# Fixed halves for the products, channel tiles added ahead of the logits, and a new order of the pieces

## The chip, the core and the metric

The kernel runs on one core of one Trainium2 chip. The core has a matmul engine (TensorE, PE in the profile; its weight loads are listed as PEld), three engines for elementwise work (VectorE or DVE, ScalarE or ACT, GpSimd or POOL), a sequencer that only issues DMAs (SyncE or SP), and 16 DMA engines. Data is worked on in SBUF, 128 partitions wide; matmuls write to PSUM, eight banks of 512 float32 values per partition. The metric is the device time of one execution in microseconds (us), median of the runs.

## The reference

The input x has 2048 rows of 640 channels. It is normalised, and two branches of it are added to x:

```
xn  = layernorm(x)                                   # per row, eps 1e-5, no scale or shift
A   = attention(xn): q, k, v = xn @ wqkv; 32 heads of 20 channels
      row i looks at rows i, i-2, i-4, ... i-14 (8 window positions, dilation 2)
      logits * 20^-0.5, positions before row 0 masked, softmax over the 8, weighted sum of v, @ wo
B   = gelu(xn @ w1 + b1) @ w2 + b2                   # 640 -> 1536 -> 640, tanh form of gelu
out = x + A + B
```

All inputs and the output are bfloat16.

## The kernel before

**Chunks.** The 2048 rows are worked on as four chunks n = 0 to 3 of 512 rows, each of four blocks of 128 rows. The 640 channels are five tiles of 128, permuted so that the four partitions of a group of 128/32 belong to one head in each of the five tiles; a head's 20 channels are 4 partitions in 5 tiles.

**The pieces of a chunk**, by the names that the order list uses (n is the chunk, further digits count parts):
- `st` (VectorE, L409/L411): mean and variance of one block of x rows, two half rows and one aggregation; `rs` (ScalarE, L430) the square root, `rc` (VectorE, L434/L436) its reciprocal. Block 1 of chunk 0 gets its sum and its sum of squares on ScalarE instead (`sm`, `nm`, `sq`).
- `xn` the normalised rows (VectorE in chunk 0, ScalarE L446 later) and `tc` their transposition into xnT: through TensorE in chunk 0 (`tp`, `tc`), by a transposing DMA on SP later (L477).
- `pj`/`pc`: a projection tile of q, k or v (second digit 0, 1, 2) on TensorE, five matmuls of 512 columns (L509), and its copy out of PSUM on ScalarE (L568). Chunk 0 does this in smaller pieces (`ga` to `ge`, `hj`, with copies `gc`, `hc`). `pad` carries the last 14 columns of k or v into the next chunk.
- `qk` (VectorE, L583): the product of q with k shifted by one window position, all five channel tiles, 2560 elements per partition. Two window positions share one of four rotating buffers `prod`. `lg` (TensorE, L608): sums the products over a head's 20 channels with the 0/1 matrix head_of, into the logits L. For every pair of window positions it runs over 5 channel tiles and 4 blocks, 256 columns each, the four blocks into four 32-partition groups of L: 80 matmuls a chunk.
- the softmax: `mk` mask (chunk 0), `m` maximum, `mx` subtraction, `ss` sums, `ri` reciprocal, `at` weights on VectorE; `ex` exp on ScalarE.
- `xd`, `xs`: DMAs (SP and ScalarE queue) that spread the weights of 32 heads over 128 partitions, into the one buffer ax.
- `av` (VectorE, L681): v times weight, per window position, into the same rotating buffers; `ad` (L690) three additions of 5120 elements and `ot` (L696) one of 2560 give oT.
- `f1`/`ge`: a tile of the hidden layer, five matmuls (L703) and the gelu on ScalarE (L714) into one of 18 buffers hT.
- `o`/`oc`/`od`: an output block of 128 rows, five pieces on TensorE (four of three hidden tiles, the last of the five tiles of oT; L734 for 512 columns, `lo`, L736 for 128, `hi`), the copy to SBUF on ScalarE (L741/L742) and an accumulating DMA on GpSimd (L747) into out. `xp` puts x into out ahead of that and `xb` adds b2. The very last block adds x on VectorE and is stored plainly (`oclo`, `ohi`, `ochi`).

**What sets the order.** Every engine runs its instructions in the order in which they were emitted. The kernel emits the pieces in the order of the list `ORDER`, for PE, DVE, ACT and SP; GpSimd's order is left to the framework. The framework puts in the waits: a piece waits for what it reads, and for the last reader of a buffer that it overwrites. PSUM has four `acc` buffers for projections and hidden tiles, two banks for L and two for lo/hi. The class Plan only names the pieces, their times and needs; the list itself is fixed.

**Loads.** SP issues, in this order, x block 0, wq, wk, x blocks 2 and 3, wv, x blocks 4 to 7, x blocks 8 to 15, w1 in two halves; `ld` later brings w2, wo and b2. Ten matmuls on constants keep TensorE busy until the first data is there.

Of the kernel before, what the change touches and what calls it, by code (L numbers as in the profile page):

```python
# [10 lines left out]
ACT = mybir.ActivationFunctionType  # L11
# [4 lines left out]
PE, VE, SE, DQ, GQ = "pe", "ve", "se", "dq", "gq"  # L16


class Plan:

    TABLE = 1.3
    LAG = {PE: 0.22, VE: 0.08, SE: 0.1, DQ: 0.0, GQ: 0.0}

    def __init__(self, offsets):  # L30
        self.offsets = offsets
        self.tasks, self.by, self.bufs, self.pools = [], {}, {}, {}

    def offset(self, name):
        kind = name[: 4 if name[:2] in ("pj", "pc", "ad") else 3]
        return self.offsets.get(kind, 0.0) + (self.offsets.get(name, 0.0) if name != kind else 0.0)

    def pool(self, name, n):
        self.pools[name] = n

    def add(self, name, engine, us, rank, needs, fn, bufs=(), after=0.0, table=None, slack=0.0, hold=0.0):
        t = {
            "name": name,
            "eng": engine,
            "us": us,
            "rank": rank + self.offset(name),
            "needs": list(needs),
            "fn": fn,
            "bufs": list(bufs),
            "after": after,  # L50
            "table": table,
            "slack": slack,
            "hold": hold,
            "i": len(self.tasks),
        }
        self.tasks.append(t)
        self.by[name] = t
        for b in bufs:
            self.bufs.setdefault(b, set()).add(name)
        return name  # L60

# [12 lines left out]
RD = float(D) ** -0.5  # L74
# [4 lines left out]

COLS = ((0, 2), (2, 4), (4, 5))  # L80
PERIOD = 52.0


ORDER = """
pad01 pad02 st00a st00 sm rs00 me nm rc00 sq xn00a xn00b tp00a tp00b tc00a rs01 tb ga tc00b rc01 xn01 gb2 b1 tp01
gb3 tc01a tc01b gb4 gd gc0 ge st03a hj101 gc4 st03 st02a rs03 hj102 st02 hc101 hj100 rs02 hc102 rc02 rc03 gc1 hj200
xn03 xn02 hc100 st11a tp03 tp02 st13a tc03 hj201 st11 tc02 st10a hj202 hc200 st12a hj012 st10 hj010 st13 hc012 hc202
st12 hj111 hc010 hc201 hj011 rs1 hc111 rc1 st21a hj110 hc011 st22a st22 hj112 hc110 st20a hj212 st33a hc112 f102
xn10 qk031 hc212 f100 xn13 tc10 qk001 ge02 f109 qk020 hj210 pad11 tc13 ge09 hj211 qk010 xn11 f108 hc211 qk000 ge00
f101 tc11 qk011 f105 ge01 ge08 qk021 f104 xn12 f1011 tc12 ge04 qk030 f1010 ge011 st23a st21 lg00 ge010 st20 ld lg01  # L90
ge05 st23 lg02 lg03 st31a rs2 pj114 mk m0 pj102 pc114 st32a st30a pj110 pc102 mx0 hc210 pj111 pc110 st32 ex0 pj101
rc2 st31 st30 pj100 st33 pj112 ss0 pc100 pc101 pj104 xn21 ri0 pj103 tc21 pc104 at0 pc111 pj113 pc103 pc112 pj123
pc113 xn23 qk120 f113 pc123 tc23 xn22 f103 qk111 pj121 ge03 qk121 f118 xd0 qk130 ge13 f107 ge18 f112 qk100 ge07
pad21 f106 ge12 qk110 xs0 f115 ge06 qk131 xw0 f110 rs3 qk101 o020 tc22 xn20 o021 ge15 lg10 lg11 av011 lg12 pc121
tc20 lg13 ge10 rc3 pj120 av000 o022 pc120 av031 xn32 o023 pj122 tc32 av021 f111 pc122 m1 xn30 pj124 ge11 av030 tc30
pad12 pj214 av020 pj204 pc214 pj203 pc204 av001 pj211 pc203 av010 pc124 pj202 xn33 mx1 pc211 pj210 tc33 xn31 ad01
pj221 pc210 pc202 pj223 tc31 pj201 ad00 pj220 pc201 pc223 pj213 xp0 pj200 pc213 ad02 pc221 pj212 pc220 pc200 pj224
pc212 ex1 xb0 ot0 pj310 f1110 qk231 pc310 o024 qk220 pj300 oc02 ss1 pad31 od02 o000 o001 qk200 o002 o003 ri1 o004
at1 pj313 qk201 xd1 oc00 o010 pc313 qk211 pc300 pj301 xs1 qk210 o011 o012 qk221 o013 xw1 pj303 qk230 o014 xp1 xb1
lg20 oc01 lg21 av130 pc303 lg22 pc224 lg23 av100 o030 f138 av110 o031 od00 ge38 av111 pj312 o032 pc301 m2 ge110 f117  # L100
pc312 av131 f116 av120 pj304 pj302 mx2 o033 pc302 av121 ge16 f121 ge17 ad11 f1111 xp2 f1210 ge21 xb2 ge111 o034
ge210 av101 pad22 pc304 f119 ad10 pj311 pj222 pc311 xb3 oc03 pj314 ad12 ge19 od01 f114 od03 f125 ge14 pc222 ot1
pj324 pad32 pc314 ex2 o100 qk331 pj322 qk321 o101 ge25 o102 ss2 o103 pj323 ri2 o104 qk330 pc323 pc322 pj320 at2 oc10
pj321 pc320 qk311 xd2 xs2 o110 pc324 qk301 o111 pc321 o112 qk310 f120 qk300 f126 xw2 f130 ge26 qk320 f127 xl lg30
ge27 lg31 av201 lg32 lg33 o113 m3 o114 av211 f1311 oc11 av200 od11 o120 o121 od10 av221 o122 av230 o123 o124 av220
f1211 oc12 mx3 od12 o130 av210 o131 ge20 ge30 f124 ex3 ad20 f123 o132 ge311 o133 av231 o134 ge24 ss3 f128 ge211 oc13
f129 ad21 ge23 f122 ge29 ge28 f131 ge22 ri3 o210 at3 f135 ad22 o211 xd3 f134 f1310 ot2 o212 ge310 ge31 o213 xs3 o214
xw3 f137 oc21 ge34 od21 o220 av311 o221 o222 av300 o223 av310 o224 f136 av321 oc22 od22 o230 av301 o231 od13 o232
av320 o233 av331 o234 av330 f132 oc23 od23 o200 ad31 o201 ge32 ge36 o202 ge37 f139 ad30 f133 ge39 ge35 o203 ge33
o204 ad32 o310 oc20 o311 o300 ot3 o301 o302 o303 o304 o312 oc30 o313 od30 o320 od20 o321 o322 o323 o314 o324 oc31  # L110
od31 o330 oc32 o331 od32 o332 o333 o334 ohi oclo ochi
""".split()


def make_plan(fns, offsets={}):

    pl = Plan(offsets)
    for name, n in (
        ("acc", 4), ("L", 1), ("O", 1), ("xnT", 3), ("q", 2), ("k", 2), ("v", 2), ("prod", 4),
        ("e", 1), ("attn", 1), ("ax", 1), ("oT", 1), ("hT", 18), ("osb", 2), ("xn", 2), ("m", 1), ("rs", 1), ("ss", 1), ("stats", 4), ("bw", 2),  # L120
    ):
        pl.pool(name, n)

    def f(kind, *a):
        return lambda: fns[kind](*a)

    def turned(n, pair=None):
        if n:
            return [f"tc{n}{bl}" for bl in range(BPC)]
        every = ["tc00a", "tc00b", "tc01a", "tc01b", "tc02", "tc03"]  # L130
        return every if pair is None else every[4 * pair : 4 + 4 * pair]

    def done(n, which):
        if n:
            return [f"pc{n}{which}{to}" for to in range(KT)]
        return (["gc0", "gc1", "gc4"] if which == 0 else [f"hc{which}0{g}" for g in range(len(COLS))]) + [
            f"hc{which}1{g}" for g in range(len(COLS))
        ]

    pl.add("tb", PE, 0.1, -99, ["tp00b"], f("tb"))  # L140
    pl.add("b1", VE, 0.1, -90, ["tb"], f("b1"))
    for n in range(NCH):
        base = n * PERIOD
        prev = base - PERIOD
        early = base + (-37.0 if n == 1 else -85.0)
        xnT, q, k, v, oT = (("xnT", n), ("q", n), ("k", n), ("v", n), ("oT", n))
        hTs = [("hT", n, ft) for ft in range(FT)]

        for bl in range(BPC):
            land = (3.2, 3.65, 9.3, 9.3)[bl] if n == 0 else (0.0, 13.3, 17.6, 17.6)[n]  # L150
            r = -40 if n else -90
            if n == 0 and bl == 1:
                pl.add("sm", SE, 0.84, -99, [], f("sum1"), after=land)
                pl.add("nm", SE, 0.22, -99, ["sm"], f("neg1"))
                pl.add("me", VE, 0.12, -98, ["sm"], f("mean1"))
                pl.add("sq", SE, 0.93, -99, ["nm"], f("sq1"))
                pl.add("rs01", SE, 0.3, -99, ["sq"], f("sqrt", 0, 1, 2), table="sqrt")
                pl.add("rc01", VE, 0.16, -99, ["rs01", "me"], f("rstd", 0, 1, 2))
                continue
            pl.add(f"st{n}{bl}a", VE, 0.42, r, [], f("st", n, bl, 0), [("stats", n, bl)], land)  # L160
            pl.add(f"st{n}{bl}", VE, 0.65, r, [f"st{n}{bl}a"], f("st", n, bl, 1), [("stats", n, bl)], 7.9 if n == 0 and bl == 2 else 0.0)
            if n == 0:
                pl.add(f"rs{n}{bl}", SE, 0.3, -100, [f"st{n}{bl}"], f("sqrt", n, bl, bl + 1), table="sqrt")
                pl.add(f"rc{n}{bl}", VE, 0.16, -99, [f"rs{n}{bl}"], f("rstd", n, bl, bl + 1))
        if n > 0:
            pl.add(f"rs{n}", SE, 0.3, -98, [f"st{n}{bl}" for bl in range(BPC)], f("sqrt", n, 0, BPC), table="sqrt")
            pl.add(f"rc{n}", VE, 0.25, early + -4.0, [f"rs{n}"], f("rstd", n, 0, BPC))
# [18 lines left out]
        if n == 1:  # L186
            pl.add("ld", DQ, 9.2, -1000, turned(1), f("ld"))
# [623 lines left out]
```

## Time and profile before

| | us |
|---|---|
| median of 3 runs | 213.07 (212.35, 213.07, 219.66) |
| span of the profiled execution, first to last instruction | 210.6 |
| its own time | not listed; the lowest run is 1.7 above the span |
| PE busy | 205.5 |
| DVE busy | 173.4 |
| ACT busy | 111.7 |
| POOL busy | 19.8 |
| last matmul ends | 207.9 |

The page gives busy time per engine, then the span cut into 40 slices with the busy share in tenths. The chain that ended last is followed back from the last instruction, at each step to what released it. A group's row reads: line, engine, operation, output from inputs, shapes, count, then busy time and mean nanoseconds of one, then the idle time of the engine ahead of it and what ended most of it. A row of the timeline reads: start, duration, engine, line, operation, output from inputs, count, and in brackets the idle time before. The granted TensorE clock was 1.00 over the whole span. PEld's busy time overlaps PE's.

### The profile page before, as it was taken

Reading aid. Unit: us, or ns where it says so; the run is one execution under the profiler, and the core shown is the slowest. Engines: PE = TensorE matmul, PEld = TensorE weight load, DVE = VectorE, ACT = ScalarE, POOL = GpSimd, SP = SyncE. Lnnn points to the kernel's source line nnn. Section 1 sums busy time; section 2 is a strip of 40 time slices with the busy share of each in tenths; the row PEclk is TensorE's granted clock in tenths of the full one; section 3 lists DMA queues with packets and bytes.
Section 4 is the critical chain, followed back from the end, with each engine's and each line's share of the span. In section 5 each row is a group of like instructions: output and inputs, shape, how many; then the busy total and the mean of one; then the engine's idle time right before and its main releaser. Section 6 shows DMA issues by size and latency. Waiting matters only on the chain.

```text
span 210.6 us, 3645 instructions
## 1 busy us (share of the span) xinstructions
PE 205.5 (98%) x1511; PEld 118.5 (56%) x1535; DVE 173.4 (82%) x178; ACT 111.7 (53%) x193; POOL 19.8 (9%) x37
## 2 busy tenths in 40 slices
PE   8999999999999999999999999999999999999994
PEld 2999656554465555555654555565554455555552
DVE  3587998969979999997899999989999829997001
ACT  5576977889786748330727487321396221441120
POOL 2000000000000002110400600101101011101130
PEclk9999999999999999999999999999999999999999
DMA  6999416924932173569296690621122571212224
GB/s 221 364 363 372 90 33 188 382 56 82 142 72 42 20 187 34 93 94 224 79 150 218 93 156 3 139 93 13 24 29 34 100 127 21 24 27 31 31 21 75
DMA packets 24072, 23.93 MB, mean 114 GB/s; under 512 B 9080, under 2 KB 21880, under 8 KB 24056
## 3 DMA queue, kind: packets, MB, share of 16 engines
q1 hardware_dynamic: 17008, 14.68, 25.1%
q0 software_dynamic: 4144, 4.92, 17.5%
q10 hardware_dynamic: 2904, 4.10, 7.0%
q8 instruction: 12, 0.20, 0.4%
q14 instruction: 4, 0.03, 0.1%
HBM read 10.00 MB, written 7.54 MB: 83 GB/s over the span
## 4 chain that ended last, share of the span: by engine, by line
PE 87%; DMA 7%; SPq 4%; issue 1%; DVE 0%
PE lo L734 27%; PE hps L703 24%; PE pps L509 23%; PE hi L736 8%; DMA w_sb<-in_B_w_dram 7%; PE L L608 4%; SPq L342 2%; SPq L359 2%; PE gps L553 1%; SPq L345 1%; DVE osb L764 0%
## 5 line engine op out<-in xcount | busy, mean ns | idle before, releaser
L703 PE MATMUL hps<-xnT,w_sb 128*128 128x512 bf16 x235 | 55.3, 379 | 0.3
L681 DVE TENSOR_TENSOR pv<-vT,ax 128x2560 bf16<-128x2560 bf16 x32 | 45.8, 1483 | 9.1 <-DMA ax<-attn 4.6
L734 PE MATMUL lo<-w_sb,hT 128*128 128x512 bf16 x184 | 52.9, 379 | 0.1
L583 DVE TENSOR_TENSOR prod<-qT,kT 128x2560 bf16<-128x2560 bf16 x32 | 45.5, 1483 | 1.9 <-ACT kT L568 1.5
L714 ACT ACTIVATE hT<-hps,b1T 128x512 bf16<-128x512 f32 x48 | 31.6, 689 | 18.4 <-PE hps L703 16.9
L736 PE MATMUL hi<-w_sb,hT 128*128 128x128 bf16 x192 | 40.3, 219 | 0.5 <-issue 0.2
L703 PEld LDWEIGHTS <-w_sb 128*128 128x128 bf16 x240 | 22.8, 98 | 26.3 <-DMA w_sb<-in_B_w_dram 0.6
L690 DVE TENSOR_TENSOR pv<-pv 128x5120 bf16<-128x5120 bf16 x12 | 33.7, 2821 | 0.2
L741 ACT CAST osb<-lo 128x512 bf16<-128x512 f32 x15 | 8.8, 587 | 44.7 <-issue 26.7
L734 PEld LDWEIGHTS <-hT 128*128 128x128 bf16 x192 | 18.7, 98 | 22.5 <-issue 0.4
L734 PE MATMUL lo<-wo,oT 128*128 128x512 bf16 x74 | 21.9, 379 | 0.0
L747 POOL DMA_DIRECT2D out_dram<-osb x15 | 13.6, 904 | 86.2 <-ACT osb L742 80.1
L736 PEld LDWEIGHTS <-hT 128*128 128x128 bf16 x192 | 18.4, 98 | 2.7
L509 PE MATMUL pps<-xnT,wk_sb 128*128 128x512 bf16 x73 | 18.2, 379 | 0.1
L509 PE MATMUL pps<-xnT,wv_sb 128*128 128x512 bf16 x72 | 18.0, 379 | 0.1
L509 PE MATMUL pps<-xnT,wq_sb 128*128 128x512 bf16 x75 | 18.0, 379 | 0.1
L736 PE MATMUL hi<-wo,oT 128*128 128x128 bf16 x80 | 16.9, 219 | 0.3
L409 DVE BATCH_NORM_STATS2 stats<-x_sb 128x6 f32<-128x320 bf16 x30 | 13.0, 467 | 4.2 <-DMA x_sb<-in_A_x_dram 4.2
L490 POOL DMA_DIRECT2D out_dram<-b2bc x4 | 5.3, 1465 | 98.6 <-DMA out_dram<-x_sb 98.6
L568 ACT CAST qT<-pps 128x512 bf16<-128x512 f32 x15 | 8.7, 590 | 8.8 <-PE pps L509 8.8
L734 PEld LDWEIGHTS <-oT 128*128 128x128 bf16 x80 | 7.8, 98 | 9.4
L509 PEld LDWEIGHTS <-wk_sb 128*128 128x128 bf16 x75 | 8.6, 118 | 7.3 <-issue 0.2
(75 smaller groups left out, 198.7 us busy)
## 6 DMA issues: line engine op xcount, KB each, us to landing
w_sb<-in_B_w_dram SPq DMA_DIRECT2D x4, 960.0 KB, 11.4
out_dram<-osb POOLq DMA_DIRECT2D x15, 160.0 KB, 3.4
ax<-attn SPq DMA_DIRECT2D x8, 256.0 KB, 4.7
ax<-attn ACTq DMA_DIRECT2D x8, 256.0 KB, 4.3
out_dram<-b2bc POOLq DMA_DIRECT2D x3, 640.0 KB, 6.6
x_sb<-in_A_x_dram SPq DMA_DIRECT2D x1, 1280.0 KB, 14.0
out_dram<-x_sb ACTq DMA_DIRECT2D x1, 1120.0 KB, 4.6
wq_sb<-in_A_wqkv_dram SPq DMA_DIRECT2D x1, 800.0 KB, 4.8
```

The costliest lines, as they stand in the source:

```text
L409: nc.vector.bn_stats(stats[:, i, :], x_sb[:, b, i * (D // 2) : (i + 1) * (D // 2)])
L509: nc.tensor.matmul(ps[:], lhsT=wqkv_p[which][:, ti, to, :], rhs=xnT[:, ti, :], start=(ti == 0), stop=(ti == KT - 1),)
L568: nc.scalar.copy(dest[:, to, off : off + CH], tiles["pps", n, which, to][:])
L583: nc.vector.tensor_tensor(out=prod[:, i, :, :], in0=qkv_tile(n, 0)[:], in1=qkv_tile(n, 1)[:, :, off : off + CH], op=ALU.mult,)
L681: nc.vector.tensor_tensor(out=pv[:, i, :, :].rearrange("p t (j c) -> p t j c", j=BPC), in0=qkv_tile(n, 2)[:, :, off : off + CH].rearrange( ...
L690: nc.vector.tensor_tensor(out=ta[:], in0=ta[:], in1=tb[:], op=ALU.add)
L703: nc.tensor.matmul(ps[:], lhsT=w1_sb[:, ti, ft * P : (ft + 1) * P], rhs=tiles["xnT", n][:, ti, :], start=(ti == 0), stop=(ti == KT - 1),)
L714: nc.scalar.activation(hT[:], tiles["hps", n, ft][:], ACT.Gelu_apprx_tanh, bias=b1T[:, ft : ft + 1], scale=1.0)
L734: nc.tensor.matmul(lo[:], lhsT=lhs, rhs=rhs[:, 0:CH], start=first, stop=last)
L736: nc.tensor.matmul(hi[:, 0 : D - CH], lhsT=lhs, rhs=rhs[:, CH:D], start=first, stop=last)
L741: nc.scalar.copy(osb[:, 0:CH], tiles["lo", n, bl][:])
L747: nc.gpsimd.dma_start(rows, tiles["osb", n, bl][:], accum_op=ALU.add)
```

## The change

Line numbers from here on that name the new kernel say so.

- **Products in fixed halves.** Two fixed buffers `half`, of four window positions each, take the place of the four rotating ones. A product (`qk`, `av`) now covers one block of 128 rows and four window positions: 4 x 5 x 128 = 2560 elements as before. The shifted operand is read through `window`, an access pattern with a step of -2 per window position; the other operand is broadcast.
- **Channel tiles added ahead of the logits.** In chunks 0, 2 and 3, four new VectorE additions `pa` of 2048 elements add channel tiles 1 to 0 and 3 to 2 in the halves; `lg` then runs over tiles 0, 2 and 4 only. A logits matmul has 512 columns (four window positions): 24 in these chunks, 40 in chunk 1. `lg` is one piece that needs all products.
- **Statistics.** For chunks 2 and 3, sum (`su`), negative mean (`ng`) and sum of squares (`sq`) come from ScalarE instead of VectorE. For all rows, the square root and reciprocal are replaced by a tiny VectorE operation (`rc`: variance plus eps) and a power of -0.5 on GpSimd (`rp`, and a product for the bias from chunk 1 on). ScalarE starts with the gelu table loaded.
- **Reuse.** Chunk 3's hidden tiles are written over wq and wk, whose last use is past. In chunks 1 and 3 the spread weights go to the SBUF rows of x blocks 0 to 6, after these were copied to out.
- **Loads.** x blocks 8 to 15 move from ahead of w1 to a piece `ldx` behind chunk 1's transposes, next to w2 (`ld2`); wo and b2 follow in `ldo`.
- **New order.** `ORDER` is another list.

```diff
+    half = [prodp.tile([P, W // 2, KT, CH], BF16, name=f"half{i}") for i in range(2)]
+    def window(src, h, cs):
+        first = PAD - DIL * (W // 2 * h) + cs.start
+        row = src[:, :, first : first + cs.stop - cs.start]
+        (part, n_part), (tile_step, n_tile), (_, n_col) = row.ap
+        return bass.AP(tensor=row.tensor, offset=row.offset,
+            ap=[[part, n_part], [-DIL, W // 2], [tile_step, n_tile], [1, n_col]])
...
+    def do_qk(n, j, h):
+        cs = slice(j * P, (j + 1) * P)
         nc.vector.tensor_tensor(
-            out=prod[:, i, :, :],
-            in0=qkv_tile(n, 0)[:],
-            in1=qkv_tile(n, 1)[:, :, off : off + CH],
+            out=half[h][:, :, :, cs],
+            in0=qkv_tile(n, 0)[:, :, cs].unsqueeze(1).to_broadcast([P, W // 2, KT, P]),
+            in1=window(qkv_tile(n, 1), h, cs),
             op=ALU.mult,
...
+    def do_pa(n, h, c):
+        cs = slice(c * 2 * P, (c + 1) * 2 * P)
+        even, odd = (half[h][:, :, i : KT - 1 : 2, cs] for i in range(2))
+        nc.vector.tensor_tensor(out=even, in0=even, in1=odd, op=ALU.add)
+    def do_lg(n):
+        ts = range(0, KT, 2 if n in PAIRED else 1)      # PAIRED = (0, 2, 3)
+        for t in ts:
+            for h in range(2):
+                for j in range(BPC):
+                    nc.tensor.matmul(
+                        L[j * H : (j + 1) * H, W // 2 * h : W // 2 * (h + 1), :],
+                        lhsT=head_of[:],
+                        rhs=half[h][:, :, t, j * P : (j + 1) * P],
...
+    def do_su(n, bl):
+        nc.scalar.activation(xn_tile(n, bl)[:], x_sb[:, n * BPC + bl, :], ACT.Identity, accum_out=col(acc, n, bl))
+    def do_ng(n, bl):
+        nc.scalar.activation(col(neg, n, bl), col(acc, n, bl), ACT.Identity, scale=-1.0 / D)
+    def do_sq(n, bl):
+        nc.scalar.activation(xn_tile(n, bl)[:], x_sb[:, n * BPC + bl, :], ACT.Square,
+            bias=col(neg, n, bl), accum_out=mv[:, n * BPC + bl, 1:2])
...
-        nc.scalar.activation(std[:, sl], mv[:, sl, 1], ACT.Sqrt, bias=eps_t[:], scale=1.0)
-        nc.vector.reciprocal(rstd[:, sl], std[:, sl])
+        nc.vector.tensor_scalar(out=ve[:, sl], in0=mv[:, sl, 1], ... op0=ALU.mult, op1=ALU.add)
+        nc.gpsimd.tensor_tensor(out=rstd[:, sl], in0=ve[:, sl], in1=expo[:, 0 : b1 - b0], op=ALU.pow)
+        if n:
+            nc.gpsimd.tensor_tensor(out=nmr[:, sl], in0=neg[:, sl], in1=rstd[:, sl], op=ALU.mult)
...
+    def ax_view(n):
+        if n % 2 == 0:
+            return get(("ax", n), lambda: axp.tile([P, BPC, W, P], BF16, tag="ax", name="ax"))[:]
+        return (x_sb[:, 0 : 2 * BPC, :].rearrange("p b d -> p (b d)")[:, 0 : BPC * W * P]
+            .rearrange("p (j w c) -> p j w c", j=BPC, w=W))
...
     def do_ge(n, ft):
-        hT = hp.tile([P, CH], BF16, tag="hT", name="hT")
+        if n < NCH - 1:
+            hT = hp.tile([P, CH], BF16, tag="hT", name="hT")[:]
+        else:
+            spent = wqkv[ft // 6][:].rearrange("p t n -> p (t n)")
+            hT = spent[:, (ft % 6) * CH : (ft % 6 + 1) * CH]
```

Parts of the two lists that the text below speaks of, the stretch around the logits of chunk 0 and the end:

```diff
-ge05 st23 lg02 lg03 st31a rs2 pj114 mk m0 pj102 pc114 st32a st30a pj110 pc102 mx0 hc210 pj111 pc110 st32 ex0 pj101
+... pj111 pj102 pj113 pc102 pj110 pc113 pc111 lg0 mask m0 mx0 ge0_6 pc110 su23 ex0 ldo xp0
+pj100 pc100 pj112 pad11 pc112 ss0 ri0 at0 xd0 pj114 pj104 pc104 pc114 pj101 pc101 pj103 pc103 ...
...
-o204 ad32 o310 oc20 o311 o300 ot3 o301 o302 o303 o304 o312 oc30 o313 od30 o320 od20 o321 o322 o323 o314 o324 oc31
-od31 o330 oc32 o331 od32 o332 o333 o334 ohi oclo ochi
+ot3 o324 oc32 o314 o300 od32 o301 o302 o303 o334 oc31 oclo o304 od31 oc30 od30 ohi ochi
```

## The prediction

> **What bounds the kernel now.** I read the engine totals first, then the slices, then the chain that ended last.
>
> ```profile
> PE 205.5 (98%) x1511; PEld 118.5 (56%) x1535; DVE 173.4 (82%) x178; ACT 111.7 (53%) x193; POOL 19.8 (9%) x37
> ...
> PE   8999999999999999999999999999999999999994
> ...
> DVE  3587998969979999997899999989999829997001
> ...
> PE 87%; DMA 7%; SPq 4%; issue 1%; DVE 0%
> ```
>
> TensorE stands for 5 us in 210.6, and from slice 2 on the chain is matmuls back to back. It ends with a short tail. So two numbers decide: how much matmul work the change takes out, and how long it makes TensorE stand still. VectorE is the second engine, at 82%; its zeros at the end are spare time that lies behind its last work, not before it. The chain also gives the step of each kind of matmul.
>
> ```profile
> 24.99 2.18 PE gps L553 x20
> ...
> 33.65 2.30 PE L L608 x80
> ...
> 36.34 10.74 PE pps L509 x49
> ...
> 59.28 2.30 PE L L608 x80
> ```
>
> 49 matmuls of 512 columns in 10.74 us are 0.219 each (a piece of five, `pj` or `f1`: 1.08). Twenty of 256 columns take 2.18, 0.109 each. Logits matmuls, 256 columns into 32 output partitions, take 2.30/80 = 0.029: four column groups run side by side at 0.115 per four. A third of an output block (`o..0` to `o..3`, three lo/hi pairs) is 0.81 and its last piece 1.36, from the steps of L734/L736.
>
> **Matmuls removed.** Before, 80 logits matmuls per chunk, 2.30. After, chunks 0, 2, 3 have 24 of 512 columns: six fours, each one 512-column step plus the 0.006 of above, 0.225: 1.35. Chunk 1 has ten fours, 2.25. Saved: 3 x 0.95 + 0.05 = 2.9 us of TensorE. If the column groups did not run side by side at 512 columns, the 24 would cost 24 x 0.219 = 5.3 instead; the 256-column row speaks against it.
>
> **VectorE.** The 64 products keep their 2560 elements; inner runs of 128 with a broadcast operand are what L681 has today, and L681 and L583 agree.
>
> ```profile
> L681 DVE TENSOR_TENSOR pv<-vT,ax 128x2560 bf16<-128x2560 bf16 x32 | 45.8, 1483 | 9.1 <-DMA ax<-attn 4.6
> ...
> L583 DVE TENSOR_TENSOR prod<-qT,kT 128x2560 bf16<-128x2560 bf16 x32 | 45.5, 1483 | 1.9 <-ACT kT L568 1.5
> ...
> L690 DVE TENSOR_TENSOR pv<-pv 128x5120 bf16<-128x5120 bf16 x12 | 33.7, 2821 | 0.2
> ```
>
> And from VectorE's timeline:
>
> ```profile
> 21.48 11.30 DVE L583 TENSOR_TENSOR prod<-qT,kT 128x2560 bf16<-128x2560 bf16 x8 [0.44 <-ACT kT L563]
> ```
>
> Eight products take 11.3, an addition of 5120 elements 2.81. A new `pa` has 2048 elements; on the line through 2560 (1.41) and 5120 (2.81) that is 1.13, twelve are 13.6 us. The statistics of eight row blocks leave (16 x 0.42 plus 8 x 0.13, 7.8 us); two tiny operations per group are exchanged for as many. VectorE: 173.4 + 13.6 - 7.8 = 179, still under TensorE as a total. The totals do not decide, the order does.
>
> **The first stretch, to the logits of chunk 1 (`lg1`).** Here VectorE's chain can be laid end to end. Rows 4 to 7 land at 13.3, as now; four blocks' statistics end at 17.4 (they start at 13.34 in the trace and end there); two tiny operations, 17.7; eight products to 29.0; four `pa` to 33.5; `lg0` to 34.9. Then the softmax:
>
> ```profile
> 36.32 1.22 DVE L621 TENSOR_REDUCE m<-L 128x128 f32<-128x1024 f32 x1
> ...
> 38.25 1.21 DVE L627 TENSOR_TENSOR L<-L,m 128x1024 f32<-128x1024 f32 x1
> ...
> 42.30 0.69 DVE L643 TENSOR_TENSOR sums<-e 128x512 f32<-128x512 bf16 x1
> ...
> 43.81 0.95 DVE L650 RECIPROCAL rs<-sums 128x128 f32<-128x128 f32 x1
> ```
>
> Mask, maximum and subtraction take 2.7 (37.6); ScalarE's table load 1.28 and exp 1.02 follow them (40.0); sums to weights are 3.7 in the trace (42.30 to 46.02), so 43.7; eight products of chunk 1 to 55.2. Today VectorE reaches that point at 58.8 (47.52 plus eight products), so it gains 3.6 us. But TensorE gets there sooner: the new list has 25 `pj`/`f1` pieces ahead of `lg1` instead of 29, no output third instead of two, and `lg0` is shorter: 4 x 1.08 + 2 x 0.81 + 0.95 = 6.9 us less. From 59.28 that gives 52.4. So TensorE waits 55.3 - 52.4 = **2.9 us**. Smaller things are inside this wait: a wait for wk (landed 8.4, wanted near 7.7); four full PSUM buffers while `ex0`, ahead of `pc100` on ScalarE, waits for VectorE (TensorE full at 39.1, released at 40.4); and, as a gain, w1, on which TensorE now waits 0.6 at 23.73 and which comes ahead of x rows 8 to 15 (3.6 us of transfer). That later load must land before ScalarE's first sum at 33 to 36; I put it at 32.
>
> **From `lg1` on, stage by stage.** Work of the two engines by the same durations:
> - end of `lg1` to `lg2`: TensorE 43 x 1.08 + 16 x 0.81 + 4 x 1.36 = 64.9. VectorE 24 products 33.9, 6 additions 16.8, 2 `ot` 2.8, softmax 6.0, 4 `pa` 4.5, seven tiny 0.9: 64.9. A tie.
> - end of `lg2` to `lg3`: 13 x 1.08 + 8 x 0.81 + 1.36 = 21.9 against softmax 6.0, 8 products 11.3, 4 `pa` 4.5: 21.8. A tie.
> - end of `lg3` to the first use of `ot2`: 12 x 1.08 + 13 x 0.81 + 3 x 1.36 = 27.6 against softmax 6.0, 1.0 of waiting for exp (2.4, one product beside it), 8 products, 3 additions, `ot`: 28.1. TensorE waits 0.5.
> - `ot3` comes 21.2 later, TensorE has 23.5: 2.3 to spare.
>
> An addition that reads what the instruction before it wrote starts about 0.1 later than one that does not (153.00 after a product that ends at 152.97, where products overlap by 0.07): 0.2 more in the ties. Sum: -2.9 + 2.9 + 0.5 + 0.2 = **0.7 us later** at TensorE's last matmul, 208.6 instead of 207.9.
>
> **ScalarE and GpSimd.** ScalarE gains eight blocks of sum, mean and square. One block took 3.62 to 5.62, 2.0 us: 16 us. It loses four table loads (1.28 each) and seven square roots: 121 us, hidden behind 98% TensorE as long as nothing in its order waits. What waits behind a late `xn` is the emptying of PSUM; by the sums above `xn33` is the closest, its `rc33` being late on VectorE (83.6) with four buffers filled at 85.7. The power replaces a square root and a reciprocal (4.46 to 4.95 for block 0), and the first matmul waits for it. The trace has no arithmetic on GpSimd: from below its 128x1 memset (0.1), from above its costliest operation (0.28); I take 0.3 with the hand-over, no change at the start. Beside VectorE it shows only DMA issues of 0.9 us (one at 93.01, inside five products of 7.09 us, the normal step), so I take 0 for what VectorE loses; the other bound is 14 instructions between `lg1` and `lg2` at 0.28, 3.9 us, all of it on the tie.
>
> The Trainium skill ("SBUF — State Buffer", Who interferes with whom) speaks against that zero: a VectorE instruction with two SBUF inputs and a GpSimd instruction that reads SBUF exclude each other for a whole instruction. No run here shows it. By the row the time is the sum below; by the rule, with VectorE held for 0.1 to 0.28 each of 14 times, it would be an estimated 1.4 to 3.9 us more, or GpSimd waits for up to a product of 1.4 us itself.
>
> **The tail.** Today, from the timeline:
>
> ```profile
> 204.34 0.86 POOL L747 DMA_DIRECT2D out_dram<-osb  x1 [0.50 <-ACT osb L742]
> ...
> 208.25 0.35 ACTq L767 DMA_DIRECT2D out_dram<-osb  x1
> ```
>
> and, from the DMA issues of the last 17 us (count, size, median us to landing):
>
> ```profile
> out_dram<-osb POOLq DMA_DIRECT2D x3, 160.0 KB, 3.5
> ...
> out_dram<-osb ACTq DMA_DIRECT2D x1, 32.0 KB, 1.5
> ```
>
> The last accumulating store starts 3.5 us before TensorE ends; the last plain one lands at 209.75, 1.85 after it, and the span closes 0.85 later. The new list puts `o304` directly ahead of `ohi` (0.95). Its copy begins at once, the store 1.05 later (203.29 to 204.34), landing 3.5 after that: 3.65 after TensorE. **1.8 us longer.** If it landed as fast as the plain one, 0.
>
> **Sum.** Span 210.6 + 0.7 + 1.8 = 213.1. The page shows no own time for this execution; the runs took 212.35, 213.07 and 219.66, so about 2.5 us lie around the span at the median, and I carry the 2.5 over: 213.07 + 2.5 = **215.6**.
>
> **Rivals.**
> - *GpSimd takes time from VectorE, or delays ScalarE's `xn`.* Place: between `lg1` and `lg2`, where 64.9 stands against 64.9. From 0.12 us per instruction on (1.7 in all) it passes 217.3; at 0.28 it is 215.6 + 3.9 = 219.5. For it: the ties. Against: the memsets at 0.1 and the unhindered products.
> - *Only TensorE's work counts.* Without the waits, 213.07 - 2.9 + 1.8 = 212.0, and 210.2 without the tail. For it: 98%. Against: the chain to 55.2, every link of which is a row.
> - *The pairing does not save matmul time*, the 24 cost what the 80 did: 215.6 + 2.9 = 218.5. Against: the four groups at 0.115.
>
> **Chances.** Forecast 0.50, first rival 0.32, second 0.12 (a quarter of it under 208.8), third 0.06. A change of 2%, 4.3 us, is about what this kernel's runs can tell. Faster by more: 0.03; within: 0.50 + 0.09 = 0.59; slower: 0.38. The range goes from 211.0 (second rival, most of it) to 220.0 (the GpSimd bound and a little).
>
> **What would show it.** Right: logits groups of 24 matmuls at 1.35; VectorE without a pause from 17.7 to 33.5; TensorE idle for about 2.9 us ahead of `lg1`, near 55.3, and almost none between `lg1` and `lg3`; the last GpSimd store landing after ScalarE's. Wrong: products or `pa` with another mean; VectorE gaps beside GpSimd arithmetic; ScalarE waiting on `xn` with TensorE stopped behind it; the x rows landing after 36.

## The result, and the profile after

The changed kernel takes 228.17 us at the median (227.15 to 228.80), the kernel before 212.78: a ratio of 1.072, 95% interval 1.069 to 1.076. It is **slower**, by some 15 us. The forecast was 215.6, the range ended at 220.0, and no rival reached the result: the dearest, GpSimd's interference, was priced at 219.5.

The first lines to read are again the engine totals, the slices and the chain, now of the page of the changed kernel (its span is 226.9, its own time 228.68, its mean granted clock 0.975).

```profile
PE 208.8 (92%) x1327; PEld 115.2 (51%) x1327; DVE 179.1 (79%) x170; ACT 118.5 (52%) x222; POOL 46.7 (21%) x59
...
PE   6899999799992999999499999999998999999990
...
PEclk9699999999998599999999999999999999999998
...
PE 46%; issue 18%; POOL 11%; DVE 7%; ACT 6%; DMA 6%; SPq 3%; ACTq 1%; POOLq 0%
```

TensorE has holes where it had none: a 2 in slice 12 (68 to 74 us; the slices are counted from 0) and a 4 in slice 19 (108 to 113), and behind the first hole the clock row drops to 8 and 5. VectorE's total is 179.1, as forecast, so the loss isn't work on VectorE. GpSimd is on the chain with 11%; before, it wasn't. The waits say who held whom (total, times, longest):

```profile
ACT xn L252 <- POOL nmr L246: 14.1, 4, 5.6
...
PE lo L564 <- ACT osb L571: 4.4, 3, 3.0
PE hps L529 <- ACT hT L544: 4.2, 1, 4.2
```

ScalarE's normalization waits for GpSimd, and TensorE waits for ScalarE. The place is found by laying the timelines of the engines side by side. GpSimd (L244 is the power, L246 the product for the bias):

```profile
64.26 0.55 POOL L244 TENSOR_TENSOR rstd<-ve,expo 128x1 f32<-128x1 f32 x1 [7.15 <-DVE ve L231]
...
65.46 5.92 POOL L244 TENSOR_TENSOR rstd<-ve,expo 128x1 f32<-128x1 f32 x1 [0.38 <-DVE ve L231]
71.46 0.19 POOL L246 TENSOR_TENSOR nmr<-neg,rstd 128x1 f32<-128x1 f32 x1
```

VectorE at the same time:

```profile
64.09 1.23 DVE L446 TENSOR_TENSOR L<-L,m 128x1024 f32<-128x1024 f32 x1
65.22 0.15 DVE L231 TENSOR_SCALAR ve<-mv 128x1 f32<-128x1 f32 x1
65.28 5.69 DVE L508 TENSOR_TENSOR half<-vT,ax 128x2560 bf16<-128x2560 bf16 x4
```

ScalarE, behind that power:

```profile
65.94 0.67 ACT L544 ACTIVATE hT<-hps,b1T 128x512 bf16<-128x512 f32 x1
71.68 0.92 ACT L252 ACTIVATE xn<-x_sb,nmr,rstd 128x640 bf16<-128x640 bf16 x1 [5.08 <-POOL nmr L246]
72.51 0.67 ACT L544 ACTIVATE hT<-hps,b1T 128x512 bf16<-128x512 f32 x1
73.19 1.28 ACT L456 ACT_TABLE_LOAD   x1
```

And TensorE, `f1` of five matmuls, which should take 1.08:

```profile
73.23 2.29 PE L529 MATMUL hps<-xnT,w_sb 128*128 128x512 bf16 x5 [4.20 <-ACT hT L544]
75.31 0.63 PE L564 MATMUL lo<-w_sb,hT 128*128 128x512 bf16 x1
...
111.41 0.38 PE L564 MATMUL lo<-w_sb,hT 128*128 128x512 bf16 x1 [3.00 <-ACT osb L571]
```

Read downwards, this is the whole chain of events. The same one-column power took 0.55 us beside VectorE's subtraction, whose large operand is in PSUM, and 5.92 beside four products, which read two operands from SBUF; it ended at 71.4, 0.4 after the last of the four, when VectorE had nothing to issue. `xn22` waited 5.08 for it. Behind `xn22` on ScalarE stood the gelu that empties a PSUM buffer, and `ex1`. TensorE filled its buffers and stopped for 4.20. Then it ran at half clock: in 73.2 to 79.0 the granted clock is 0.52, which costs 2.8 us more. Near 105 it happens again: the power (104.50) takes 3.07 and the product behind it 2.28, over two additions; `xn31` waits 5.60, `oc03` stands behind it, and TensorE stops for 3.00 at 108.4, the last row above (that stop left the clock at 1.00).

Laid beside the prediction, stage by stage (the profiled execution, differences in us):

| | forecast | measured | later |
|---|---|---|---|
| `lg1` starts | 55.3 | 56.32 | 1.0 |
| `lg1` to `lg2`, start to start | 67.3 | 78.14 | 10.8 |
| `lg2` to `lg3` | 23.3 | 23.42 | 0.1 |
| `lg3` to TensorE's end | 62.7 | 63.9 | 1.2 |
| TensorE's end to the span's end | 4.5 | 5.2 | 0.7 |
| around the span | 2.5 | 1.8 | -0.7 |

One stage holds nearly all of it, and in it 4.20 + 0.28 + 3.00 of stops and 2.8 of clock make 10.3.

### The profile page after: what moved, and what is told of

The parts are those of the page before. It is cut to its first block, busy times and chain, and to the rows that moved or that the text cites. A ratio compares the mean times of both kernels' runs of the same rounds, so it can differ in the third digit from the quotient of the medians.

```text
span 226.9 us, 3292 instructions
## 1 busy us (share of the span) xinstructions
PE 208.8 (92%) x1327; PEld 115.2 (51%) x1327; DVE 179.1 (79%) x170; ACT 118.5 (52%) x222; POOL 46.7 (21%) x59
## 4 chain that ended last, share of the span: by engine, by line
PE 46%; issue 18%; POOL 11%; DVE 7%; ACT 6%; DMA 6%; SPq 3%; ACTq 1%; POOLq 0%
PE lo L564 13%; PE hps L529 12%; PE pps L313 11%; POOL rstd L244 6%; DMA out_dram<-x_sb 5%; PE hi L566 3%; DVE half L397 3%; POOL out_dram L577 2%; POOL nmr L246 2%; PE gps L357 2%; ACT xn L252 2%; PE gps L326 2%; SPq L154 2%; PE L L424 1%; DMA x_sb<-in_A_x_dram 1%
## 5 line engine op out<-in xcount | busy, mean ns | idle before, releaser
L529 PE MATMUL hps<-xnT,w_sb 128*128 128x512 bf16 x240 | 56.1, 384 | 4.2 <-ACT hT L544 4.2
L564 PE MATMUL lo<-w_sb,hT 128*128 128x512 bf16 x144 | 42.7, 389 | 4.5 <-ACT osb L571 4.4
L397 DVE TENSOR_TENSOR half<-qT,kT 128x2560 bf16<-128x2560 bf16 x32 | 45.7, 1482 | 0.8 <-ACT kT L367 0.8
L566 PE MATMUL hi<-w_sb,hT 128*128 128x128 bf16 x144 | 32.1, 223 | 0.0
L244 POOL TENSOR_TENSOR rstd<-ve,expo 128x1 f32<-128x1 f32 (+1 forms) x13 | 20.9, 1607 | 36.5 <-DVE ve L231 31.8
L508 DVE TENSOR_TENSOR half<-vT,ax 128x2560 bf16<-128x2560 bf16 x16 | 23.0, 1481 | 2.5 <-PE L L424 2.5
L564 PEld LDWEIGHTS <-hT 128*128 128x128 bf16 x144 | 14.4, 100 | 17.9 <-issue 1.7
L508 DVE TENSOR_TENSOR half<-vT,x_sb 128x2560 bf16<-128x2560 bf16 x16 | 22.6, 1483 | 0.0
L517 DVE TENSOR_TENSOR half<-half,half 128x5120 bf16<-128x5120 bf16 x8 | 22.2, 2820 | 0.1
L252 ACT ACTIVATE xn<-x_sb,nmr,rstd 128x640 bf16<-128x640 bf16 x12 | 11.0, 923 | 14.1 <-POOL nmr L246 14.1
L566 PEld LDWEIGHTS <-hT 128*128 128x128 bf16 x144 | 14.4, 100 | 7.2 <-issue 5.9
L415 DVE TENSOR_TENSOR half<-half 128x2048 bf16<-128x2048 bf16 x12 | 14.0, 1216 | 0.0
```

Of the source, the lines that this page charges most:

```text
L244: nc.gpsimd.tensor_tensor(out=rstd[:, sl], in0=ve[:, sl], in1=expo[:, 0 : b1 - b0], op=ALU.pow)
L252: nc.scalar.activation(xn[:], x_sb[:, i, :], ACT.Identity, bias=col(nmr, n, bl), scale=col(rstd, n, bl))
L397: nc.vector.tensor_tensor(out=half[h][:, :, :, cs], in0=qkv_tile(n, 0)[:, :, cs].unsqueeze(1).to_broadcast([P, W // 2, KT, P]), in1=window ...
L415: nc.vector.tensor_tensor(out=even, in0=even, in1=odd, op=ALU.add)
L508: nc.vector.tensor_tensor(out=half[h][:, :, :, cs], in0=window(qkv_tile(n, 2), h, cs), in1=ax_view(n)[:, j, ws, :].unsqueeze(2).to_broadca ...
L517: nc.vector.tensor_tensor(out=a, in0=a, in1=b, op=ALU.add)
```

## The experiments

**Theory:** GpSimd's small operations are held up while VectorE runs operations with two SBUF operands; what costs is what stands behind ScalarE's `xn`. **Rivals:** GpSimd takes time from VectorE; the new start and order are slow by themselves; the statistics overload ScalarE; the pairing or the tail costs more than I had summed.

**Power off GpSimd** (e1), and **power beside, unread** (e2).

```diff
-        nc.gpsimd.tensor_tensor(out=rstd[:, sl], in0=ve[:, sl], in1=expo[:, 0 : b1 - b0], op=ALU.pow)
-        if n:
-            nc.gpsimd.tensor_tensor(out=nmr[:, sl], in0=neg[:, sl], in1=rstd[:, sl], op=ALU.mult)
...
+        nc.vector.tensor_scalar(out=rstd[:, sl], in0=ve[:, sl], scalar1=-0.5, scalar2=1.5, op0=ALU.mult, op1=ALU.add)
+        if n:
+            nc.vector.tensor_tensor(out=nmr[:, sl], in0=neg[:, sl], in1=rstd[:, sl], op=ALU.mult)
```

> The changed kernel, but the power and the product for the bias are taken off GpSimd: VectorE computes one Newton step from 1 (1.5 - 0.5 v) right behind rc, and the bias product. That is not the power -0.5, only near it while the variance is near 1; its cost is two tiny VectorE operations per group. Theory (GpSimd's small operations are starved by runs of two-input VectorE operations, ScalarE's xn waits for them, PSUM isn't emptied, TensorE stops and loses its clock): lg1 to lg2 shrinks from 75.8 us to about 65, so 228.2 - 10.9 = 217.3, between 215.5 and 219.0, and no ScalarE xn waits more than 1 us for its scale. Rival, start and order: lg1 to lg2 keeps its 75 us, 226 to 228. Rival, load of the ScalarE statistics: ScalarE still holds TensorE up after lg1, 222 or more.

> As the kernel without GpSimd's power, but GpSimd still computes all powers and products at the same places, into buffers that nobody reads. Theory (only the wait for the result costs): within 1.0 us of the kernel without them, with GpSimd powers again stretched from 0.55 us to several us beside VectorE products, and products still 1.48 us. Rival (GpSimd takes time away from VectorE, as I had bounded it at 0.28 us per instruction): 3 to 10 us slower than the kernel without them, with longer products.

e1, e2 and e3 scale the rows without the power: their formula is near it only for variances near 1. The instructions that follow have the same shapes, so the times can be compared.

Measured: e1 218.62 (218.57 to 218.66), e2 219.04 (218.95 to 219.30). Without GpSimd's power 9.6 us are gone; with the power back but unread, 0.4 return, all of them ahead of the first logits, where VectorE waits 0.41 for x rows at 13.34, which it doesn't in e1. `lg1` to `lg2` in e1, TensorE:

```profile
55.70 2.39 PE L425 MATMUL L<-half,head_of 128*32 128x512 bf16 x40
...
124.31 1.48 PE L425 MATMUL L<-half,head_of 128*32 128x512 bf16 x24 [0.69 <-DVE half L416]
```

68.6 instead of 78.1 us. (`xn` still waits up to 1.7 for VectorE's tiny operations, not under 1 as expected.) In e2, GpSimd beside the same products, additions (82.49, 2.82) and all:

```profile
65.84 0.55 POOL L249 TENSOR_TENSOR rstd_g<-ve,expo 128x1 f32<-128x1 f32 x1 [0.76 <-DVE ve L233]
66.47 1.13 POOL L251 TENSOR_TENSOR nmr_g<-neg,rstd_g 128x1 f32<-128x1 f32 x1
82.28 0.56 POOL L249 TENSOR_TENSOR rstd_g<-ve,expo 128x1 f32<-128x1 f32 x1 [8.09 <-DVE ve L233]
82.92 2.44 POOL L251 TENSOR_TENSOR nmr_g<-neg,rstd_g 128x1 f32<-128x1 f32 x1
```

My expectation missed one thing here: the powers themselves weren't stretched, since VectorE's two tiny operations gave them 0.4 us of room; the products behind them were, from 0.19 to the end of the VectorE instruction in progress. VectorE's products and additions kept their means (1479 to 1483 and 2820 ns). So GpSimd takes nothing measurable from VectorE; only waiting for it costs. (The stretched powers of the changed kernel say the same: there too the products take 1481 to 1483 and the additions 2820 ns.) The rival "start and order" falls with e1: it can hold no more than what e1 still has over the kernel before.

**One part alone** (e4): the kernel before with GpSimd's power.

```diff
-        nc.scalar.activation(std[:, sl], mv[:, sl, 1], ACT.Sqrt, bias=eps_t[:], scale=1.0)
...
-        nc.vector.reciprocal(rstd[:, sl], std[:, sl])
...
+        nc.vector.tensor_scalar(out=std[:, sl], in0=mv[:, sl, 1], scalar1=EPS, scalar2=None, op0=ALU.add)
...
+        nc.gpsimd.tensor_tensor(out=rstd[:, sl], in0=std[:, sl], in1=expo[:, 0 : b1 - b0], op=ALU.pow)
```

> The kernel before, with only this part of the change: in place of ScalarE's square root and VectorE's reciprocal, VectorE adds eps and GpSimd computes the power and the product for the bias, for all rows, at the places of the square roots. Theory: only groups beside runs of products are stretched (that of chunk 3, and no more than one or two); four ScalarE table loads go; 212 to 215. Rival (the power is slow or costly wherever it stands): 216 or more.

212.83 against 212.44, ratio 1.001 (0.997 to 1.006). The power is harmless there: chunks 1 to 3 have one operation each for their four row blocks, and only that of chunk 3 falls beside a product, 2.25 instead of 1.02:

```profile
57.80 2.25 POOL L436 TENSOR_TENSOR rstd<-std,expo 128x4 f32<-128x4 f32 x1 [20.59 <-DVE neg L435]
```

**Room on VectorE**, at every group (e5) and at two of them (e14). More work for a busy engine, as a test of the cause:

```diff
+        if n:                                  # e14: if (n, b0) in ((2, 2), (3, 1)):
+            for _ in range(2):
+                nc.vector.memset(room[:], 0.0)
```

> The changed kernel with GpSimd's power as it is, but VectorE fills a scratch buffer twice (two memsets of 128x256 f32) behind every rc of chunks 1 to 3, before its next product or addition: work that reads nothing, so that GpSimd can read while it runs. Theory: the powers behind it fall to 0.55 to 1.0 us, no ScalarE xn waits more than 2 us for GpSimd, TensorE no longer stops for 3 to 4 us, and the time falls although VectorE has more to do: 217.3 to 223, by the price of the memsets (about 0.5 us for a pair by 1 element per 0.96 ns, 4 us for eight groups on VectorE's chain). Rival (GpSimd's power is slow whatever VectorE does, or ScalarE's load holds TensorE up): 227 or more.

> The changed kernel in its own order, with room on VectorE (two memsets, 0.66 us) behind rc22 and rc31 only, the two places whose powers held ScalarE for more than 5 us. Theory: 1.3 us of VectorE's time buys back most of what the eight groups bought in the run with room everywhere (228.2 to 221.3), and 4 us of memsets less are on VectorE's chain: 219, between 217.5 and 221. Rival (the other stretched powers matter as much): 222 to 226.

e5: 221.29 (221.10 to 221.53), 6.9 us faster than the changed kernel although VectorE has 18 memsets more (0.66 a pair; no run shows the 0.96 ns per element that the expected 0.5 was worked out with). TensorE's longest stop behind `lg1` is 1.8, but one `xn` still waits 4.4 for GpSimd, not under 2 as expected: the products for the bias are now the ones held up. GpSimd, beside the memsets and then the four products:

```profile
66.19 0.55 POOL L248 TENSOR_TENSOR rstd<-ve,expo 128x1 f32<-128x1 f32 x1 [1.03 <-DVE ve L232]
66.82 1.33 POOL L250 TENSOR_TENSOR nmr<-neg,rstd 128x1 f32<-128x1 f32 x1
```

e14: 221.69 (220.89 to 222.66) with four memsets. That is 6.5 us for 1.3 us of VectorE, so the two places where ScalarE waited longest held two thirds of the loss. It wasn't the 219 I expected, and no faster than e5: a stop of 2.23 near 88 is new, for a copy of vT that stands behind `xn33`, which waits 4.5 for GpSimd. Its waits:

```profile
ACT xn L256 <- POOL nmr L250: 13.4, 5, 4.5
```

ScalarE waits for GpSimd 13.4 us in all, against 14.1 in the changed kernel, and the kernel is 6.5 us faster. The sum of a wait says little; what stands behind it decides.

**Other order on ScalarE** (e10, e13), **the same with the earlier store** (e11), **the changed kernel again** (e9). GpSimd stays as it is:

```diff
-rp22 xn22 tc22 pj123 f11_10 ge1_10 ex1 ss1
+rp22 pj123 f11_10 ge1_10 ex1 xn22 tc22 ss1
-f12_4 xn31 tc31 rc32 rp32 oc03 o010
+f12_4 rc32 rp32 oc03 xn31 tc31 o010
```

> The changed kernel, GpSimd's power and all work as they are, but on ScalarE the two xn that waited longest go behind what they held up: xn22 behind ge1_10 and ex1, xn31 behind oc03. Theory (GpSimd's delay costs only by what stands behind it on ScalarE): TensorE's stops of 4.2 and 3.0 us and the lower clock behind them go, about 10 us: 218.5, between 217 and 221, with powers as long as before. Rival (the stops have other causes, or a late xnT stops TensorE instead): 225 or more.

> The changed kernel, unaltered, profiled a second time: is the power that lasted over four products (5.9 us, begun near 65.5) a fixed feature or one draw? Theory: the same instructions are stretched, by the rest of at least the one VectorE instruction that runs when they begin; whether this one again lasts for four products is open, and if it lasts for one only (about 1.7 us) the time is some 4 us under 228.

> The kernel with the two xn moved, and also o304 ahead of o332, o333 and o334. By the 1.9 us that this edit of the tail was worth in the kernel without GpSimd's power, and the 218.5 above: 216.6, between 215 and 219. The kernel before stays ahead.

> The kernel with xn22 and xn31 behind what they held up, profiled again: what its 221.0 us still hold above 218.5. Theory: the stops of 4.2 and 3.0 us are gone, but the late xn22 now makes chunk 2's xnT late, and TensorE waits 2 to 5 us for its transposing load near 77. Rival (the rest is VectorE's chain): no stop of TensorE above 1.5 us after 60.

e10: 220.73, 220.81 and 221.28. A fourth execution, the profiled one, took 763.73, with 1.10 us instead of 0.38 for TensorE's matmuls of 512 columns from end to end; its trace shows no cause, and nothing is read from it. e13, the same kernel, took 220.96 when profiled and 225.60 in an execution without a trace. So an exchange of neighbours on ScalarE, with all work and GpSimd's instructions left alone, gives back some 7 us, at the upper edge of what I expected.

Not all of that is the theory's second half, since the length of the first power is not fixed. e9 took 227.95, and its 5.93 at 65.42 repeats the 5.92. But in e13 and in e11 it reads, beside the same four products (the 6.53 also through the sum that follows them):

```profile
65.12 1.72 POOL L244 TENSOR_TENSOR rstd<-ve,expo 128x1 f32<-128x1 f32 x1 [0.38 <-DVE ve L231]
```

```profile
65.79 6.53 POOL L244 TENSOR_TENSOR rstd<-ve,expo 128x1 f32<-128x1 f32 x1 [0.38 <-DVE ve L231]
```

In e13 the first place was helped by a power 4.2 us shorter as well, and the two effects aren't separated there. In e11 the execution with the 6.53 took 224.2, the three others, which have no trace, 218.45 to 218.84. With the 1.9 that the earlier store was worth without the power (e6, below), the order alone was worth some 2 us in that execution (224.2 against 228.2 - 1.9): the stop for the gelu was gone, but the late `xn22` made chunk 2's transposed rows late, and TensorE stopped for them.

```profile
76.81 3.93 PE L313 MATMUL pps<-xnT,wq_sb 128*128 128x512 bf16 x10 [4.74 <-DMA xnT<-xn]
```

In e13, with 1.72, this stop is 1.41: by size the rival (no stop above 1.5) holds in e13, and the theory in e11. The cleaner test of the second half is the second place, where e13's power and product take 3.07 and 2.28 as in the changed kernel: there the stop of 3.00 for `oc03` is gone, and one of 1.08 for a gelu is left.

What e13 has beyond e1 (2.3 us) is in the same stage, 70.8 from `lg1` to `lg2` instead of 68.6: besides these two stops, VectorE is idle for 1.37 and 0.42 while `rc` waits for ScalarE's squares, which now come later.

**The tail** (e6), and **a stop inside another wait** (e12), both without GpSimd's power:

```diff
-o301 o302 o303 o334 oc31 oclo o304 od31 oc30 od30 ohi ochi             # o332, o333 earlier in the list
+o301 o302 o303 oc31 o304 od31 oc30 od30 o332 o333 o334 oclo ohi ochi
```

```diff
-su23 ex0 ldo xp0 pj100 pc100 pj112 pad11 pc112 ss0
+su23 ldo xp0 pj100 pc100 pj112 pad11 pc112 ex0 ss0
```

> The kernel without GpSimd's power (rstd on VectorE as 30 - 4000 v, one Newton step from 20, near the power -0.5 for variances near 0.0025), and the end of the list changed: o304 goes ahead of o332, o333 and o334, so that its accumulating store starts 2.35 us earlier before TensorE's last matmul (3.3 instead of 0.95). Theory: the store no longer ends the span; from 218.6 to 216.3, between 215.8 and 217.0. Rival (something else ends there, or ot3 is late without the two thirds ahead of it): 217.8 or more.

> The kernel without GpSimd's power and with the earlier o304 (216.7), and ex0 goes behind pc100 and pc112 on ScalarE, so that TensorE's stop of 1.34 us at 41 (four full PSUM buffers while ex0 waits for VectorE) goes. Theory (VectorE's chain sets lg1, this stop lies inside the wait for it): the stop goes, TensorE then waits for VectorE inside lg1 instead, and the time stays within 0.5 us of 216.7. Rival (TensorE's own stops set lg1): 215.4.

e6: 216.69 (216.11 to 217.63), 1.9 us less than e1; the spans are 216.6 and 214.1. In e1 the last accumulating store is issued at 211.68, 0.1 after TensorE's end, in e6 at 209.12, before TensorE's end and before the plain store (ACTq). The first line is e1's, the others e6's:

```profile
211.68 0.86 POOL L578 DMA_DIRECT2D out_dram<-osb  x1 [4.84 <-ACT osb L573]
```

```profile
209.12 0.86 POOL L578 DMA_DIRECT2D out_dram<-osb  x1 [3.76 <-ACT osb L573]
...
211.74 0.35 ACTq L598 DMA_DIRECT2D out_dram<-osb  x1
```

e12: 216.49 against 216.69, no difference. The stop of 1.34 at 41 is gone, and in its place TensorE waits in `lg1`:

```profile
56.16 2.12 PE L425 MATMUL L<-half,head_of 128*32 128x512 bf16 x34 [1.00 <-DVE half L398]
```

So VectorE's chain sets `lg1`, and TensorE's own stop lay inside the wait.

**The pairing**, left out of the change (e3) and put alone into the kernel before (e8):

```diff
-PAIRED = (0, 2, 3)
+PAIRED = ()
```

```diff
+        if made[n, wp] == 2 and n in PAIRED:
+            even, odd = (prod[:, :, k : KT - 1 : 2, :] for k in range(2))
+            nc.vector.tensor_tensor(out=even, in0=even, in1=odd, op=ALU.add)
...
+        logits(L, tiles["qk", n, wp], wp, range(0, KT, 2 if n in PAIRED else 1))
```

> As the kernel without GpSimd's power, but no channel tiles are added ahead of the logits: the 12 additions pa go, the logits of all chunks take 40 matmuls. By my steps VectorE loses 13.6 us of work and TensorE gains 2.85 us: the wait ahead of lg1 (2.9) goes and the ties become TensorE's, so about 217.3 - 2.9 + 2.85 = 217, between 215.5 and 218.5. If VectorE is later than I summed in other stages too, 213 to 215. If pairing was a plain gain for TensorE, 219 to 220.

> The kernel before, with only the pairing: behind every second product of chunks 0, 2 and 3 VectorE adds channel tiles 1 to 0 and 3 to 2 in the rotating buffer (2048 elements), and the logits run over tiles 0, 2, 4: 48 matmuls of 256 columns instead of 80. TensorE loses 3 x 0.92 = 2.8 us, VectorE gains 13.6. Theory (the exchange is worth it only where VectorE has 4.5 us to spare): VectorE of the kernel before arrives at lg1 with TensorE and has little to spare in the middle, so 213 to 217. If VectorE has the time, 210.0.

e3: 220.63 (220.13 to 221.47), 2.0 slower than e1, beyond my 218.5: the pairing is a plain gain there. Without it TensorE simply takes 0.95 longer per chunk (`lg2` to `lg3` 24.28 instead of 23.43), and VectorE's spare 4.5 us buy little. e8: 224.13, 11.6 slower than the kernel before, far over my 217. In that order VectorE has nothing to spare ahead of the logits (waits of TensorE for the additions, total, times, longest):

```profile
PE L L615 <- DVE prod L595: 9.9, 6, 2.5
```

The pairing pays only together with the rest of the change.

**Statistics back on VectorE** (e7), without GpSimd's power:

```diff
-ACT_STATS = (2, 3)
+ACT_STATS = ()        # in the list: su -> st..a, sq -> st.., ng left out
```

> The kernel without GpSimd's power (rstd on VectorE as 30 - 4000 v), and the statistics of chunks 2 and 3 back on VectorE at the places that ScalarE's sums and squares have in the list: VectorE gains 7.8 us of work, ScalarE loses 16. By my ties VectorE is what decides between lg1 and lg2, so most of it costs: 222 to 226. Rival (ScalarE's statistics hold up TensorE through PSUM): less than 218.

227.01 (226.97 to 227.37), 8.4 slower than e1. All of it lies between `lg1` and `lg2` (77.0 us instead of 68.6), where VectorE, with 7.8 us more to do, runs without a pause from 59.4 on. TensorE's stops, the longest of 3.70, lie inside that time:

```profile
92.59 0.61 PE L565 MATMUL lo<-wo,oT 128*128 128x512 bf16 x1 [3.70 <-DVE oT L523]
```

So ScalarE's statistics were a good trade. With them in place (e1) no stop of TensorE above 0.25 us between `lg1` and `lg2` is for ScalarE; that rival falls.

No version beats the kernel before; e4 equals it. Of those built on the change the nearest are e12 and e6 (216.5 and 216.7, both with an approximation in place of the power that is near it only for variances near 0.0025), and with the power itself e11 (218.7).

## Why the prediction was wrong

**The step that failed** is in "ScalarE and GpSimd": "I take 0.3 with the hand-over", and "the other bound is 14 instructions between `lg1` and `lg2` at 0.28, 3.9 us, all of it on the tie". Three things in it were wrong.

- *The size.* A free power of one column takes 0.55, of four 1.02, the product 0.19. The 0.28 of the costliest GpSimd row before was not an upper bound: that was another operation, the one that builds the identity.
- *The direction.* I priced what VectorE loses to GpSimd. It loses nothing (e2). GpSimd loses to VectorE, from 0.55 to 1.73 beside a product, 3.07 and 3.13 beside an addition, and 5.9 over four products (the changed kernel's rows).
- *The consequence.* I had written that ScalarE is hidden "as long as nothing in its order waits", and named `xn33` as the closest. It was `xn22`, with a gelu and `ex1` behind it, and `xn31`, with `oc03` behind it. A delay of 5 us on an engine that is busy for half the span became a stop of 4.2 on the engine that decides, and 2.8 more by its clock. e1 and e14 show this for both places, e13 for the second. In e14, with the other two out of the way, `xn33` does stop TensorE, for 2.23.

The Trainium skill ("SBUF — State Buffer", Who interferes with whom) had been weighed and set aside: a VectorE instruction with two SBUF inputs contends with a GpSimd instruction that reads SBUF, and one with at most one such input, outside the two-port modes, doesn't. The runs agree with both: 0.55 beside the subtraction on PSUM and beside memsets, the whole rest of the instruction beside products and additions. They go beyond it where four products in a row held the power up to their end or longer (5.92, 5.93, 6.53), though at the same place once only for the first (1.72). Of the other half of "exclude each other", VectorE held by GpSimd, they show no sign: in e2 a power of four columns ran from 17.73 to 18.75, the first product began beside it at 17.97, and the four products took their usual 5.69. My estimate from the page went up to one product, 1.4, and stopped at GpSimd; the queue behind it was never followed.

**The first rival** had the right pair of engines in its title, "or delays ScalarE's `xn`", but only VectorE's loss in its price, 219.5. The range fell with it.

**Matmuls removed:** right. The next work starts 1.41 after a group of 24 (34.38 to 35.79; forecast 1.35), and `pa` steps are 1.14 (forecast 1.13).

**VectorE's total:** 179 forecast, 179.1 measured; 1483 per product as before.

**First stretch:** VectorE's chain to 55.3 came out at 56.1: 0.4 late at the first product (18.10), 0.8 behind the last `pa` (34.3), 1.2 behind the weights (44.9); my links add up to 55.0, not 55.2. "No change at the start" was wrong too: TensorE stands 1.14 us before its first transposition and then runs at a clock of about 0.73, VectorE's first product waits 0.48 for a copy of kT, and without GpSimd's power (e1) the first logits begin 0.62 earlier. The x rows landed near 36.4 instead of 32, one of the signs I had named for being wrong; ScalarE waited 1.00 for them, but then still waited for VectorE ahead of its exp, so they cost nothing here. The wait of 2.9 was too long: TensorE wasn't ready at 52.4; in e12, without its stop at 41, it began `lg1` at 54.4 and waited 1.0; in the changed kernel it doesn't wait there at all. The end of the stage was nearly right all the same, since VectorE sets it.

**The ties:** right to about 1.3 us. With GpSimd out of the way (e1) the tie between `lg1` and `lg2` took 68.6, against 67.3, with VectorE busy from 58.1 to 124.2 without a pause, among it some 2 us of its additional tiny operations (six groups, each 0.44 from the start of `ve` to the next work, where the changed kernel needs 0.06 to 0.12); `lg2` to `lg3` 23.4 against 23.3.

**The last stage:** 1.1 and 1.2 longer than summed in e1 and the changed kernel, of which two waits for PSUM behind `oc` (0.79 and 0.63 in e1) are most; I had counted none.

**The tail:** right in cause, short in size: 1.8 forecast, 2.5 measured (5.2 instead of 2.7 from TensorE's end to the span's). The store is issued 0.1 after TensorE's end, as forecast, and the span ends 5.0 after it, not 4.4.

With e1 the remaining difference to the forecast is 3.0 us (218.6 against 215.6): 0.4 at `lg1`, 1.3 in the tie, 0.1 between `lg2` and `lg3`, 1.1 in the last stage, 0.6 in the tail, less 0.5 around the span.

**Open** is why four products in a row starve the power to their end in some executions and not in others, and why a run of `qk` products let it in after the first (1.73 at 49.23) in the same trace. Whether the new order on ScalarE makes the short power more likely is open too: six executions of the old order took 227.15 us or more, and of the nine of the new one whose times can be used only two were over 222 (224.2 and 225.6).

## What to carry to other kernels

A small operation on a side engine is priced with what may run beside it, not alone: look up what the main engine does at that moment, and whether both read SBUF. Then follow the queue: what stands behind the instruction that waits, who needs that, and how many buffers of slack there are until TensorE stops. Moving the waiter behind what others need cost two lines of the list here and gave 7 of the 10 us, a part of it, in the one trace that shows it, through a power that happened to be short; with a long one it gave 2. Giving the side engine 0.66 us of room at two places gave 6.5.

## What the runs showed of the hardware

- GpSimd's power on 128x1: 0.55 us free, up to 6.53 beside VectorE's products; VectorE's durations don't change (products 1481 to 1483 ns, additions of two SBUF operands 2820 ns).
- Stops of TensorE of 4.20 us (changed kernel), 4.74 (e11) and 3.70 (e7) were followed by 3 to 6 us at a granted clock near half (0.52 over 5.8 us behind the first, over 5.4 behind the last); one of 3.00 wasn't. The length of a single stop doesn't decide it alone: in e8 stops of 1.03 and 2.15, with 0.5 us of matmuls between them, were followed by 3.3 us at 0.50, and 0.30 and 2.15, about as close together, weren't.
- At the start, the stop of 1.14 us between the warming matmuls and the first transposition was followed by a clock of 0.72 to 0.75 until 12 us, and in e9 one of 1.30 likewise; in e8, after 0.95, it stayed at 1.00.
